# Closing the first token group of batch 0 out of SBUF, and regrouping the work around it, in a one-core FFT-mixing and MLP kernel

## The chip, the cores and the metric

The kernel runs on one core of a Trainium2 chip. The metric is the device time of one launch in microseconds; the time before is the median of five runs. A core has five engines with one instruction queue each: TensorE (PE, with its weight loads listed as PEld), VectorE (DVE), ScalarE (ACT), GpSimd (POOL) and SyncE (SP), which here only issues DMAs. POOL and ACT issue DMAs too. Every engine takes its instructions strictly in the order in which they were written; a waiting instruction holds up all that stand behind it.

## The reference, cut to what matters

```python
X = np.fft.rfft(x, axis=1)                    # x: 8 batches, 3136 tokens, 256 channels
y = np.fft.irfft(X * (filt_r + 1j * filt_i), n=3136, axis=1)   # one filter value per frequency and channel
h = y.transpose(0, 2, 1) @ U @ V              # U: 3136 x 32, V: 32 x 3136, mixes tokens
u = y + h.transpose(0, 2, 1)
out = u + np.maximum(u @ w_ch1, 0.0) @ w_ch2  # 256 -> 1024 -> 256 channels
```

Inputs and output are float32; the kernel computes in float16 with float32 accumulation.

## The kernel before, in words

The transform of length 3136 is split as 64 x 49. **Stage 1** (`st1`) is a transform of length 64 as a matmul with the constant `wf`; its result goes by DMA to a buffer `ct1` in DRAM and comes back transposed as tiles `a2` (`load_a2`). **Stage 2** is a matmul with `w2t` over the other factor. The result, in PSUM, is multiplied by the filter tiles `fb` and `fc`. **Stage 3** transforms back (`stage3`, constant `g3`), is copied to SBUF tiles `esb` (`out3`, ACT), and goes to a second DRAM buffer `ct2`, from which it returns transposed as tiles `e2` (`load_e2`, issued by SP). **Stage 4** (`stage4`) is the last transform, a matmul with `sv`. The low-rank product U V costs little here: `uh` (U transformed, made once by `u_hat`) times `esb` gives a 32 x 256 tile (`low_rank`, `low_rank_end`), which `put_h` writes into rows 64 to 95 of each `e2` tile, and V stands in the same rows of `sv`. So stage 4 gives u, transposed, in tiles `ut`.

The tokens of a batch are cut into six groups of 512 (and a remainder of 64, which two batches share). The **main loop** walks over the groups in 8 steps each. In a step `mm1` makes 128 of the 1024 hidden channels (two matmuls, one ACT activation into the ring `hring`), `stage4` prepares the next group in two of the steps, and `mm2_part` multiplies the hidden channels of the group before by `w2sb`, adds the residual (matmuls with `idn`) and stores the output. There are 52 such groups, so 416 steps.

Stages 1 to 3 of the coming batches are laid between the steps by a planner: `at(step, function)` hangs work behind a step, `early[step]` puts it ahead. `plan_mid` places stages 2 and 3 of a batch: per index k (8 of them) a load `fetch`, the matmul `two`, three DVE multiplications `mul` (into `ta` and twice into `tb`) with an addition on POOL, or, for some k, all on POOL after an ACT copy (`pooled`), then `three`. `plan_rest` places `load_e2`, `low_rank` and `put_h`; `plan_st1` places stage 1 of the batch after, in 13 units (`step1`).

Batch 0 has nothing to hide behind. Ahead of the loop its x is transformed straight into a transposed form (`turned`, `turn_a2`), with no DRAM in between; `mid_first` then runs stages 2 and 3 in 16 half units j with another form of the filter product: one multiplication per unit (L400 on DVE, or for j = 7, 9, 12, 14 an ACT copy L395 and POOL L397), and two matmuls with different constants in stage 3. After it come the loads of `e2` for the first two groups, the low-rank product, the whole of stage 1 of batch 1 (13 units, L266 with copies L271 and L273), six `keep_warm` matmuls, stage 4 of group 0 and the copies of the filters into the form that the other batches need (`make_fa`, L543 to L549).

In the listing, POOL's queue begins with U, x of batch 0 and the filters, then V, `w1sb`, x of batch 1 and `w2sb`; SP's with `wf`, `sv` and `kr`.

Of the kernel before, what the change touches and what calls it, by code (L numbers as in the profile page):

```python
# [24 lines left out]
def _consts():  # L25
# [10 lines left out]
    wf = np.zeros((128, 25, 128))  # L36
    for h in range(2):
        wf[h::2, 0:24, 64 * h:64 * h + 64] = t1[:, 24 * h:24 * h + 24]
    wf[0:64, 24, 0:64] = t1[:, 48]
# [59 lines left out]
    return (wf.reshape(128, 25 * 128).astype(f16), w2.astype(f16), g3.astype(f16),  # L99
# [4 lines left out]
def kernel(  # L104
# [13 lines left out]
    names = ("wf", "w2", "g3", "s4", "su", "tw", "kr")  # L118
    wf_d, w2_d, g3_d, s4_d, su_d, tw_d, kr_d = (
# [22 lines left out]
    def bank(tag):  # L142
        of = {"m": (0, 1), "o": (2, 3), "w": (4,), "e": (7,), "f": (0, 1, 2, 3, 4, 7), "e0": (7, 4), "f0": (0, 1), "w1": (7, 5, 6)}[tag]
        turn[tag] = turn.get(tag, -1) + 1
        return psum[:, of[turn[tag] % len(of)], :]


    NH = 17
    hring = cst.tile([128, NH, 512], F16, name="hring")
# [3 lines left out]
    wf = cst.tile([128, 25, 128], F16, name="wf")  # L153
    for c in range(4):
        i = slice(8 * c, min(8 * c + 8, 25))
        nc.sync.dma_start(wf[:, i], wf_d.rearrange("p (i m) -> p i m", m=128)[:, i])
# [3 lines left out]
    def load_x(b, c, after=None):  # L160
# [3 lines left out]
        else:  # L164

            t = sb.tile([128, 4, XW], F16, tag="x", bufs=4, name="x")
            if after is not None:
                nc.gpsimd.tensor_copy(t[0:1, 0, 0:1], after[0:1, 0:1])
# [10 lines left out]
    def load_filters(a, z):  # L179
        n = min(z, 31) - a  # L180
        for p0, src in ((0, filt_r), (64, filt_i)):
            nc.gpsimd.dma_start(
                fb[p0:p0 + 25, a:a + n, :],
                dram(src.tensor, (a + 1) * DM, [[64 * DM, 25], [DM, n], [1, DM]]))
            nc.gpsimd.dma_start(
                fb[p0 + 25:p0 + NR, a:a + n, :],
                dram(src.tensor, (63 - a) * DM, [[64 * DM, 24], [-DM, n], [1, DM]]))
        if z == NK:
            for p0, src in ((0, filt_r), (64, filt_i)):
                nc.gpsimd.dma_start(fb[p0 + 25:p0 + NR, 31, :],  # L190
                                    dram(src.tensor, 32 * DM, [[64 * DM, 24], [1, DM]]))
            nc.gpsimd.dma_start(fb[0:25, 31, :], dram(filt_r.tensor, 0, [[64 * DM, 25], [1, DM]]))
            nc.gpsimd.dma_start(fb[65:89, 31, :],
                                dram(filt_i.tensor, 64 * DM, [[64 * DM, 24], [1, DM]]))
            nc.gpsimd.dma_start(fb[64:65, 31, :],
                                dram(filt_r.tensor, 1568 * DM, [[DM, 1], [1, DM]]))

    zero = cst.tile([128, 64], F16, name="zero")
    nc.vector.memset(zero, 0.0)
    nc.vector.memset(fb[96:128], 0.0)  # L200
    nc.scalar.copy(fb[32:64].rearrange("p s (k f) -> p (s k) f", f=64),
                   free(zero, 32, 64, 0, [[0, NK * DM // 64], [1, 64]]))
    nc.vector.memset(fc[:, 24:29, :], 0.0)
    usb = hflat[0:64, 0:NR * RANK]
    nc.gpsimd.dma_start(usb, moe_U.rearrange("(q r) p -> q (r p)", q=NQ))
# [4 lines left out]

# [7 lines left out]
    nc.scalar.dma_start(g3, g3_d.rearrange("p (f m) -> p f m", f=6))  # L218

# [3 lines left out]
    w2sb = cst.tile([128, 8, DM], F16, name="w2sb")  # L223
    vnat = hflat[64:96, 4704:4704 + SEQ]
    nc.gpsimd.dma_start(vnat, moe_V)
    nc.gpsimd.dma_start(w1sb, moe_w_ch1.rearrange("(h dd) c -> dd h c", h=2))

    sv = cst.tile([96, SEQ], F16, name="sv")
    kr = cst.tile([128, 96], F16, name="kr")

    def keep_warm(n):
        z = bank("f")
        for _ in range(n):
            nc.tensor.matmul(z, wf[:, 0, :], wf[:, 0:4, :].rearrange("p i m -> p (i m)"),
                             start=True, stop=True)
# [4 lines left out]
    def u_hat():  # L240
        ud = hflat[0:64, 1568:4704].rearrange("q (p c r) -> q p c r", c=2, r=NR)
        for p, eng in ((0, nc.vector.tensor_copy), (16, nc.scalar.copy)):
            eng(ud[:, p:p + 16], bass.AP(tensor=usb.tensor, offset=usb.offset + p,
                                         ap=[list(usb.ap[0]), [1, 16], [0, 2], [RANK, NR]]))
        for p in range(0, RANK, 8):
            z = bank("f")
# [4 lines left out]
            t = [sb.tile([98, NK, 8], F32, tag=tag, bufs=3, name="ut") for tag in ("ta", "tb")]  # L251
# [8 lines left out]
    def st1(b):  # L260
        for c in range(3):
            asb = sb.tile([128, 8, DM], F16, tag="asb", bufs=3, name="asb")
            for j in range(4):
                pf = bank("w" if b > 1 else "w1")
# [5 lines left out]
                if b == 1 and j % 2:  # L270
                    nc.vector.tensor_copy(dst, pf)  # L271
                else:
                    nc.scalar.copy(dst, pf)  # L273
                if j < 3:
                    yield
            for h in range(2):
                nc.sync.dma_start(dram(ct1[b], (16 * c + h) * 64 * DM,
                                       [[DM, 64], [128 * DM, 8], [1, DM]]), asb[64 * h:64 * h + 64])
            if 1 < b < NB - 1 and c:
                load_x(b + 1, c - 1)  # L280
            yield
        pf = bank("w" if b > 1 else "w1")
        nc.tensor.matmul(pf[0:64, 0:DM], wf[0:64, 24, 0:64], xt[b, 3], start=True, stop=True)
        al = sb.tile([64, DM], F16, tag="al", bufs=2, name="al")
        nc.scalar.copy(al, pf[0:64, 0:DM])
        nc.sync.dma_start(dram(ct1[b], 48 * 64 * DM, [[DM, 64], [1, DM]]), al)
        if 1 < b < NB - 1:
# [5 lines left out]
    cm = fc.rearrange("p s d -> p (s d)")  # L293

    def turned(c):
        for g in range(0, 8 if c < 3 else 1, 4):
            for hh in range(2):
                z = bank("f")
                n, o = 512, 3136 * hh + (8 * c + g) * 128
                if c < 3:  # L300
                    for i in range(4):
                        nc.tensor.matmul(z[:, 128 * i:128 * i + 128],
                                         xt[0, c][:, (g + i) // 2, DM * (i % 2) + 128 * hh:DM * (i % 2) + 128 * hh + 128],
                                         wf[:, 8 * c + g + i, :], start=(i == 0), stop=True,
                                         skip_group_check=True)
                else:
                    n = 64
                    nc.tensor.matmul(z[:, 0:n], xt[0, 3][:, 128 * hh:128 * hh + 128],
                                     wf[0:64, 24, 0:64], start=True, stop=True)
                if hh:  # L310
# [3 lines left out]


    esb = {}
# [6 lines left out]
    def out3(b, k, half, pe):  # L323
        if half == 0:
            esb[b, k] = sb.tile([98, 4, DM], F16, tag="esb", bufs=10, name="esb")
        nc.scalar.copy(esb[b, k][:, 2 * half:2 * half + 2, :].rearrange("p s d -> p (s d)"),  # L326
                       pe[0:98])
        if half:
            nc.sync.dma_start(dram(ct2[b], 4 * k * 98 * DM, [[DM, 98], [98 * DM, 4], [1, DM]]),
                              esb[b, k])  # L330

    def stage3(pe, parts, special):

        for n, (v, m, ms) in enumerate(parts):
            kw = dict(start=(n == 0), stop=(n == len(parts) - 1))
            if special:
                nc.tensor.matmul(pe[0:98, 0:DM], g3[:, m, :], v[:, 0:DM], skip_group_check=True, **kw)
        if special:
            for n, (v, m, ms) in enumerate(parts):
                nc.tensor.matmul(pe[0:98, DM:2 * DM], g3[:, ms, :], v[:, DM:2 * DM], start=False,  # L340
                                 stop=(n == len(parts) - 1), skip_group_check=True)
        else:
            for n, (v, m, ms) in enumerate(parts):
                nc.tensor.matmul(pe[0:98], g3[:, m, :], v, start=(n == 0), stop=(n == len(parts) - 1))  # L344
# [8 lines left out]

    def mid_first():
# [3 lines left out]
        def turn_a2(k):  # L358
            z = bank("f0").bitcast(F16)
            for i in range(4):  # L360
                for hh in range(2):
                    nc.tensor.transpose(z[:, DM * i + 128 * hh:DM * i + 128 * hh + 128],
                                        free(fc, 0, 128, 3136 * hh + 4 * k + i, [[32, 128]]), idn)
# [4 lines left out]
            if k in (1, 3):  # L368
                nc.vector.tensor_copy(a2[k], z[0:98])
            else:  # L370
                nc.scalar.copy(a2[k], z[0:98])

        todo = []

        def do3(j, uv):
            pe = bank("e0")
            stage3(pe, [(uv[:, 0], 2, 4), (uv[:, 1], 3, 5)], j == 15)
            out3(0, j // 2, j % 2, pe)

        for k in range(4):  # L380
            turn_a2(k)
        for c in range(4):
            load_x(1, c)
# [384 lines left out]
```

## Time and profile before

| What | us |
|---|---|
| median of 5 runs (553.0 to 560.42) | 556.28 |
| the profiled execution's own time | 553.0 |
| its span, first to last instruction | 551.2 |
| PE busy in the span | 515.0 (93%) |
| ACT / DVE / POOL busy | 390.7 / 352.9 / 282.4 |
| first multiplication of `mid_first` (L400) | at 24.46 |
| last matmul of stage 3 of batch 0 ends | at 45.78 |
| first matmul of the main loop (L488, step 0) | at 57.29 |
| PE held for group 0 of batch 1 (stage 4, in step 46) | 122.4 to 125.96 |

All times of single instructions count from the span's start. A row of a timeline reads: start, duration, engine, line, operation, tiles, number of instructions, and in brackets the idle time before it and what ended it. "PEclk" is the share of full TensorE clock that was granted.

### The profile page before, as it was taken

To read this page: it belongs to the slowest core of one execution; us is meant where nothing else is said; L and a number is where in the kernel's file an instruction comes from. 1 tells how busy PE (TensorE), PEld (TensorE's weight loads), DVE (VectorE), ACT (ScalarE), POOL (GpSimd) and SP (SyncE) were. 2 spreads that over 40 slices of the span, in tenths; PEclk is the share of its full clock that TensorE was granted. 3 is DMA by queue.
4 is the path that set the end of the run, shared out by engine and by line. 5 is a ranking of instruction groups with operands and counts; after the bars stand their busy time and mean duration, and the time that the engine had idled before them with its cause. 6 is when DMAs were issued, how large, how long until landed. Compare 5 with 4: busy or idle time off the path is not lost.

```text
span 551.2 us, 11638 instructions
## 1 busy us (share of the span) xinstructions
PE 515.0 (93%) x4491; PEld 374.7 (68%) x4491; DVE 352.9 (64%) x409; ACT 390.7 (71%) x684; POOL 282.4 (51%) x194
## 2 busy tenths in 40 slices
PE   5976598988999999999999999999999999999996
PEld 2733366765776777777786777777776777777775
DVE  6764864864746875858746876768656887543332
ACT  8576778764777688677777678668767677766663
POOL 5787379933891185806683195807453287300000
PEclk9899999997999999999999999999999999999999
DMA  9998988886769369865878459865654554343212
GB/s 193 165 174 185 228 180 209 193 197 176 177 160 247 117 174 231 163 201 153 198 196 205 138 174 240 164 205 145 190 151 135 142 156 122 106 116 113 96 78 87
DMA packets 85432, 92.06 MB, mean 167 GB/s; under 512 B 6741, under 2 KB 69416, under 8 KB 85376
## 3 DMA queue, kind: packets, MB, share of 16 engines
q1 hardware_dynamic: 67968, 75.12, 46.2%
q0 software_dynamic: 16960, 15.91, 19.1%
q8 instruction: 35, 0.57, 0.4%
q10 hardware_dynamic: 448, 0.28, 0.3%
q14 instruction: 21, 0.17, 0.1%
HBM read 57.42 MB, written 49.77 MB: 194 GB/s over the span
## 4 chain that ended last, share of the span: by engine, by line
PE 66%; POOL 15%; DMA 7%; DVE 7%; ACT 3%; issue 2%; DVEq 0%; POOLq 0%; ACTq 0%; SPq 0%
PE psum L521 24%; PE psum L488 24%; POOL y L634 4%; PE psum L344 4%; PE psum L352 3%; PE psum L477 3%; PE psum L497 3%; PE psum L266 3%; DMA x<-in_x_dram 2%; POOL x L170 2%; POOL tb L632 2%; POOL tb L630 2%; POOL ta L628 2%; DVE ut L482 1%; DVE tb L632 1%
## 5 line engine op out<-in xcount | busy, mean ns | idle before, releaser
L492 ACT ACTIVATE hring<-psum 128x512 f16<-128x512 f32 (+1 forms) x416 | 237.7, 576 | 104.2 <-PE psum L488 103.0
L488 PE MATMUL psum<-ut,w1sb 128*128 128x512 f16 (+1 forms) x832 | 241.1, 372 | 3.5 <-ACT hring L492 1.7
L521 PE MATMUL psum<-w2sb,hring 128*128 128x256 f16 x1536 | 231.4, 274 | 0.0
L634 POOL TENSOR_TENSOR y<-ta,tb 128x1024 f16<-128x1024 f16 x56 | 120.6, 2160 | 159.2 <-DVE tb L632 115.5
L521 PEld LDWEIGHTS <-hring 128*128 128x128 f16 x1536 | 143.7, 98 | 62.6 <-issue 2.9
L482 DVE CAST ut<-psum 128x512 f16<-128x512 f32 x96 | 71.0, 740 | 106.9 <-PE psum L477 86.6
L488 PEld LDWEIGHTS <-w1sb 128*128 128x128 f16 x832 | 104.9, 145 | 26.1 <-issue 9.1
L529 DVE COPY och<-psum 128x512 f32<-128x512 f32 x96 | 66.1, 688 | 47.5 <-PE psum L497 46.9
L326 ACT CAST esb<-psum 98x512 f16<-98x512 f32 x128 | 74.7, 586 | 19.9 <-PE psum L344 14.1
L628 DVE TENSOR_TENSOR ta<-psum,fb 128x1024 f16<-128x1024 f32 x41 | 49.9, 1217 | 7.9 <-PE psum L352 6.9
L273 ACT CAST asb<-psum 128x512 f16<-128x512 f32 x78 | 45.7, 589 | 12.3 <-PE psum L266 11.2
L497 PE MATMUL psum<-idn,ut 128*128 128x128 f16 x392 | 54.0, 219 | 0.0
L477 PEld LDWEIGHTS <-e 96*128 96x128 f16 x768 | 35.6, 98 | 25.2 <-issue 9.5
L630 DVE TENSOR_TENSOR tb<-psum,fc 64x1024 f16<-64x1024 f32 x41 | 50.3, 1226 | 0.9
L632 DVE TENSOR_TENSOR tb<-psum,fc 64x1024 f16<-64x1024 f32 x41 | 49.9, 1218 | 0.8
L477 PE MATMUL psum<-sv,e 96*128 96x64 f16 x768 | 38.7, 194 | 6.3 <-DMA e<-ct 3.5
L344 PE MATMUL psum<-y,g 128*98 128x512 f16 x105 | 39.9, 380 | 2.8 <-POOL y L634 1.4
L497 PEld LDWEIGHTS <-ut 128*128 128x128 f16 x392 | 38.4, 98 | 4.9
L628 POOL TENSOR_TENSOR ta<-pc,fb 128x1024 f16<-128x1024 f16 x15 | 32.4, 2157 | 10.8 <-ACT pc L638 10.8
L352 PE MATMUL psum<-a,w2t 98*128 98x512 f16 x113 | 34.3, 379 | 3.6 <-DMA a<-ct 2.5
L266 PE MATMUL psum<-x,wf 128*128 128x256 f16 x168 | 31.3, 273 | 2.8 <-DVE asb L271 1.0
L630 POOL TENSOR_TENSOR tb<-pc,fc 64x1024 f16<-64x1024 f16 x15 | 31.8, 2122 | 1.2
(93 smaller groups left out, 368.9 us busy)
## 6 DMA issues: line engine op xcount, KB each, us to landing
out_dram<-och SPq DMA_DIRECT2D x47, 512.0 KB
ct<-esb SPq DMA_DIRECT2D x64, 196.0 KB
x<-in_x_dram POOLq DMA_DIRECT2D x48, 256.0 KB, 8.3
e<-ct SPq DMA_DIRECT2D x48, 256.0 KB
a<-ct SPq DMA_DIRECT2D x56, 196.0 KB
ct<-asb SPq DMA_DIRECT2D x42, 256.0 KB
wf<-wf SPq DMA_DIRECT2D x3, 256.0 KB
w1sb<-in_moe_w_ch_dram POOLq DMA_DIRECT2D x1, 512.0 KB, 6.0
```

The source lines that it names most:

```text
L326: nc.scalar.copy(esb[b, k][:, 2 * half:2 * half + 2, :].rearrange("p s d -> p (s d)"), pe[0:98])
L477: nc.tensor.matmul(pu[:, 64 * i:64 * i + 64], e2[b, c][:, i, 128 * dh:128 * dh + 128], sv[:, 64 * r:64 * r + 64], start=(i == 0), stop=Tru ...
L482: nc.vector.tensor_copy(o, v)
L488: nc.tensor.matmul(ph[:, 0:n], w1sb[:, dh, :, t], gr.ut[:, dh, 0:n], start=(dh == 0), stop=(dh == 1))
L492: nc.scalar.activation(h[:, 0:n], ph[:, 0:n], RELU)
L497: nc.tensor.matmul(o[:, dh * 128:dh * 128 + 128], gr.ut[:, dh, t0:t0 + n], idn, start=False, stop=(dh == 1), skip_group_check=True)
L521: nc.tensor.matmul(o, gr.h[tt][:, i * 128:(i + 1) * 128], w2sb[:, tt, :], start=(tt == 0), stop=False, skip_group_check=True)
L529: nc.vector.tensor_copy(gr.och[:, 2 * y:2 * y + 2, :].rearrange("p j d -> p (j d)"), gr.pc)
L628: eng.tensor_mul(ta, p, va)
L630: eng.tensor_mul(tb[0:64], p[64:128], vb[64:128])
L632: eng.tensor_mul(tb[64:128], p[0:64], vb[0:64])
L634: nc.gpsimd.tensor_add(ys[k], ta, tb)
```

## The change: what it does

- **Ahead of the loop.** U is read in float32 by SP rather than converted by POOL's DMA. `wf` comes in half its size and is widened by two DVE multiplications with a 0/1 column. The zero rows of `fb` are written by one DVE memset instead of one on DVE and a 7.02 us ACT copy. The transposed tiles of batch 0 get a buffer of their own (`cm`). `u_hat` is cut into parts between the `turned` calls.
- **POOL's queue.** x of batch 0 first, then filters, V, `w1sb`, the last filter rows, x(1,0) and x(1,1); the copy of V into `sv`; after `mid_first` x(1,2), `w2sb` (now with padded rows, 512 bytes each), x(1,3), and five filter copies. x(2) is read in steps 13 to 16, x(3) in steps 40 to 45.
- **mid_first.** 15 of the 16 multiplications on DVE, only j = 12 on POOL; `low_rank_part` follows each k.
- **Group 0.** Rows 0 to 47 of e2(0,0) (k = 0 to 5) are loaded from `ct2` as soon as k = 5 is stored. The other 16 rows don't go through DRAM: `pick` gathers them from `esb` with 0/1 matrices `sel` into `zp`, and one matmul per half with `s4x` adds their part of stage 4. The low-rank part is a separate matmul.
- **Stage 1 of batch 1.** Three units stand ahead of step 0, the other ten in steps 0 to 8, on two PSUM banks of their own; eight of the copies are on DVE. The last stores to `ct1` are issued by POOL.
- **Batch 1.** Its stages 2 and 3 run in steps 15 to 42 instead of 5 to 40; k = 0, 1 and 7 use the one-multiplication form of batch 0 (`two_q`, `mul_q`, `three_q`), k = 3 and 5 run on POOL. The filter copies are cut into eight parts and spread over POOL and DVE.
- Filter products run over 113 instead of 128 partitions; batch 2 has k = 1, 3, 5 on POOL instead of 2, 5.

```diff
+    usb = hflat[0:64, 0:2 * NR * RANK].bitcast(F32)
+    nc.sync.dma_start(usb, moe_U.rearrange("(q r) p -> q (r p)", q=NQ))
+    nc.sync.dma_start(wfc, wf_d)
...
+    nc.vector.memset(fb[32:64], 0.0)
...
+        def low_rank_part(k):
+            for i in range(4):
+                a = 4 * k + i
+                nc.tensor.matmul(ph[32 * i:32 * i + 32], uh[:, a, :], esb[0, k][:, i, :],
+                                 start=(k == 0), stop=(k == 7), skip_group_check=True)
+        def pick(j):
+            for i in range(2):
+                sl = 2 * (j - 12) + i
+                for g in range(4):
+                    nc.tensor.matmul(zp[32 * g:32 * g + 32], sel[:, g, 28 - 4 * sl:60 - 4 * sl],
+                                     esb[0, j // 2][:, 2 * (j % 2) + i, :], start=(sl == 0),
+                                     stop=(sl == 7), skip_group_check=True)
...
+                if k == 5:
+                    load_e2(0, 0, 48)
+                if k == 6:
+                    load_e2(0, 1, 48)
+                if k == 7:
+                    load_e2(0, 1, 64, 48)
+                    nc.sync.dma_start(sv[0:64, 512:], s4_d[:, 512:])
+                    load_e2(0, 2)
...
-            if j in (7, 9, 12, 14):
+            if j == 12:
...
+                for k in (3, 2, 5):
+                    make_fc(k, nc.gpsimd.tensor_copy)
...
+        step1(1)
+        step1(1)
+        pick(14)
+        low_rank_part(7)
+        pick(15)
...
+        for dh in range(2):
+            nc.tensor.matmul(pu[dh], zs[:, 128 * dh:128 * dh + 128], s4x, start=False, stop=False,
+                             skip_group_check=True)
+        step1(1)
...
     mid_first()
-    load_e2(0, 0)
-    load_e2(0, 1)
...
-    for n, _ in enumerate(st1(1)):
...
-    keep_warm(6)
-    stage4(groups[0], 0)
-    stage4(groups[0], 1)
...
+    load_x(1, 2)
+    nc.gpsimd.dma_start(w2sb[:, :, 0:DM], moe_w_ch2.rearrange("(cc t) e -> cc t e", t=8))
+    load_x(1, 3)
+    for k in (4, 0, 1, 6, 7):
+        make_fc(k, nc.gpsimd.tensor_copy)
...
+            for k, q in ((0, 11), (3, 11), (1, 11), (5, 11), (2, 17), (4, 20), (6, 22), (7, 25)):
+                at(q, fetch, k)
+            for k, q, d in ((3, 17, 26), (5, 21, 32), (2, 23, 34), (4, 28, 37), (6, 33, 39)):
+                at(q, two, k)
...
+            for k, qs in ((0, (15, 16)), (1, (19, 20)), (7, (38, 39))):
+                for half, q in enumerate(qs):
+                    at(q, two_q, k, half)
...
+            return 42
...
+    for n in (0, 0, 1, 1, 2, 4, 5, 6, 7, 8):
+        at(n, step1, 1)
+    at(13, lambda: load_x(2, 0, a2q[0][0:1, 0:1]))
+    for c in range(4):
+        if c:
+            at(13 + c, load_x, 2, c)
+        at((40, 42, 44, 45)[c], load_x, 3, c)
+    for n, k in ((5, 0), (5, 1), (7, 2), (8, 3), (8, 4), (9, 5), (11, 6), (11, 7)):
+        at(n, make_neg, k)
+    for n, k in ((12, 2), (12, 3), (13, 4), (13, 5), (14, 6)):
+        at(n, make_fa, k, nc.vector.tensor_copy)
+    for n, k in ((34, 0), (35, 1), (41, 7)):
+        at(n, make_fa, k, nc.gpsimd.tensor_copy)
```

## The prediction

> **What bounds the kernel now.** I read the page's row of slices first, then the busy time by stretches cut where the stages change, then the chain of waits in the two stretches where PE is not full.
>
> ```profile
> PE   5976598988999999999999999999999999999996
> PEclk9899999997999999999999999999999999999999
> DMA  9998988886769369865878459865654554343212
> ```
>
> PE is full from about slice 10 on: nothing gains there that doesn't take work off PE. It is not full in the first five slices (0 to 69 us) and in slice 9 (124 to 138 us), where the clock drops too. The stretches (length, then busy us of PE, PEld, DVE, ACT, POOL, granted clock, DMA share, GB/s):
>
> ```profile
> 0.00:24.46 24.46, 17.16 (x135) 11.40 (x136) 16.79 (x25) 16.83 (x12) 15.98 (x31) 0.86 1.05 186
> 24.46:45.78 21.32, 17.21 (x98) 9.35 (x98) 14.29 (x13) 15.52 (x23) 17.96 (x20) 1.00 1.03 174
> 45.78:57.29 11.51, 7.17 (x82) 4.45 (x81) 5.68 (x8) 7.96 (x13) 5.92 (x1) 1.00 0.73 188
> 57.29:68.20 10.91, 6.08 (x42) 3.25 (x39) 9.88 (x18) 8.11 (x11) 4.96 (x8) 0.93 0.88 219
> 68.20:121.83 53.63, 50.99 (x431) 36.41 (x430) 35.27 (x38) 41.61 (x76) 42.33 (x25) 0.98 0.87 203
> 121.83:131.90 10.07, 6.12 (x42) 3.78 (x39) 6.18 (x8) 2.28 (x5) 0.00 (x0) 0.66 0.42 101
> 131.90:500.00 368.10, 363.37 (x3245) 269.25 (x3244) 248.31 (x279) 271.07 (x499) 195.21 (x111) 1.00 0.64 171
> ```
>
> They are: the start, bound by DMA (share 1.05); `mid_first`; the handover to the loop; group 0 (DVE 9.88 of 10.91); steps 8 to 46, near PE's limit; the stall for batch 1; the steady part. The chain shows the two handovers:
>
> ```profile
> 46.02 1.08 PE psum L416 x32
> ...
> 54.35 1.46 PE psum L234 x6
> ...
> 55.83 0.42 PE psum L477 x8
> ...
> 57.49 0.73 DVE ut L482
> ...
> 115.83 6.37 DMA ct<-esb
> ...
> 122.34 3.48 DMA e<-ct
> ...
> 125.96 0.60 PE psum L477 x8
> ```
>
> After the low-rank matmuls (46.02) ten microseconds pass with stage 1 of batch 1 before stage 4 of group 0. The second handover is a store (6.37) and a load (3.48) on which PE waits. Who sets the first one if stage 1 leaves it, SP's rows tell:
>
> ```profile
> 30.00 16.79 SPq L329 DMA_DIRECT2D ct<-esb  x8
> 52.13 1.10 SPq L438 DMA_DIRECT2D e<-ct  x2
> ```
>
> The last store is out at 46.8 and the load leaves at 52.13: 5.3 us.
>
> **The parts.** All sums are made against the profiled execution: 553.0, span 551.2.
>
> *Start, to the first multiplication: -2.3 us.* Until the last x tile (which POOL saw at 18.36) the queues moved about 200 GB/s. `wf` loses 0.41 MB and `sv`'s 0.40 MB wait, against 0.2 MB more for U and 0.18 MB for `sel` and `s4x`: 0.43 MB less, 2.1 us; x leaves POOL 0.7 us earlier; filter pieces that slip in earlier take some back. I take the last x at 17.0. Behind it the two extra `turn_a2` go (-1.2 us), but a part of `u_hat` stands on DVE there (1.08 + 0.42): first multiplication at 22.2. Bounds 0 and -4.
>
> *mid_first: -0.4.* 15 DVE multiplications at 1.22 plus one 0.69 copy are 19.0; with gaps of 0.68 as at the POOL units of before, and stage 3 of the last unit, 20.9 instead of 21.32. Losing three POOL units at 2.12 thus gains little: DVE takes their place. Its end: 43.1.
>
> *First handover: 11.51 becomes 6.9, -4.6.* The load of 48 rows hangs on j = 11, whose `esb` is stored at about 40.6. The store takes between 2.2 (the small store `al` of before, out at 60.36, its reader off at 62.6) and 5.3; I take 3.0, because the 5.3 ran through a backlog (the queues fell idle only at 51), while here some 7.3 MB, at 200 GB/s, are through by 39. Load 3.5 (row of 122.34): 47.1. Then 16 small matmuls 0.45, `s4x` 0.86, a unit of stage 1 0.22, the low-rank matmuls 0.43, the copy 0.73, and 0.2 of issue: step 0 at 50.0, not 57.29. The path beside it (`pick`, `low_rank_part`, two copies of 0.37, `kr`) ends at 45.6 and is hidden; the three stage 1 units need x(1,0) by 43, which those 7.3 MB include. Bounds: 48.5 and 52.3.
>
> *Group 0: 10.91 becomes 9.5, -1.4.* DVE gets seven stage 1 copies (0.69), two `ut` copies (0.73), two `put_h` (0.69) and three `make_neg` (half of L544's 0.69): 8.7 us. ACT loses its filter copies (1.89 each) and PE's ten units (2.2 us) fit beside. Three arrivals stand close: the second group's e2(0,1), whose last 16 rows pass a store, a load, a store and a load on SP in a row (about 53.7, needed in step 4 at 54); x(1,2), behind one multiplication and three copies on POOL; and w2sb behind it. A POOL copy of 49 x 1024 has no row; L634 with two inputs takes 2.12 and is the upper bound, DVE's 0.35 the lower; I take 1.6, nearest to L634. Then x(1,2) leaves at about 46 and w2sb at 48, needed in step 8 at 59.5. Before, w2sb took 14.7 from issue to landing behind seven x transfers (1.6 MB, some 8 us); here one tile stands ahead: about 9. Five more copies (8 us) stand ahead of batch 1's last stores on POOL; their chain (3 us out, 3.9 back) ends at 65, step 15 comes at 66.9. At 2.12 a copy it costs 2.1 us.
>
> A row bears on POOL and DVE working side by side: while POOL's 6.94 us copy (L562, to 51.71) ran, DVE's `put_h` took 0.89 instead of 0.68. The Trainium skill (SBUF — State Buffer, "SBUF: two separate sides") calls the port pair of the two an exclusive lock: the later one waits for the whole instruction. By that rule some five DVE copies of group 0 would each wait up to one POOL copy, about half on average, and the time would be some 4 us higher. I keep the row, 0.2 us each.
>
> *Steps 8 to 46: 53.63 becomes 53.2.* The one-multiplication form of k = 0, 1, 7 costs PE four more 0.215 matmuls per k: +2.6. Against it: the 2.64 us in which PE was not busy, mostly waiting for ACT and for POOL's additions; one pooled k less (8.5 us of POOL) and 5 us less of ACT copies should give back 2.0; and the clock of 0.67 in 65 to 70 us, worth 1.0 after 68.2. Bounds -2 and +3.
>
> *Second handover: +2.2.* Stage 3 of batch 1 now ends in step 42, not 40, while stage 4 stays in step 46; two steps at 1.1. The way itself (115.02 to 125.96, 10.9 us) I leave: x(3,0) and three `fetch` are issued right ahead of that store and load the queues as x(3) did before. Bounds: -2 (the store at 2.2) and +4.
>
> The Trainium skill (DMA: Bandwidth & Descriptors, "Anatomy of one DMA") gives a DMA as 2.0 us plus bytes over 436 GB/s, an estimate of 2.5 us for this 196 KB store. The rows say 5.3 and 6.37, under load. By the page the second handover would be 3.9 us shorter and the first 1.5, and the time about 544.
>
> *Steady part: 0.* The work is the same; 113 partitions don't change an instruction's length that a row would show, and batch 2's third pooled k finds POOL at 195 of 368 us.
>
> Sum: -2.3 - 0.4 - 4.6 - 1.4 - 0.4 + 2.2 = -6.9. The profiled execution would take 546.1. The median lies 3.3 above the profiled run, so I set the median at **549.3**, rounded to 549.
>
> **Rivals.**
> - *Clean handovers (0.24).* Both stores land in 2 to 3 us. For: DMA share 0.64 later, and 0.05 at 51 to 52 us. Against: 1.04 at 112 to 120. Gain 6.9 + 1.5 + 3.9: 544 (541 to 545.5).
> - *The gain is given back (0.18).* Store at 5.3 (+2.3), POOL copies at 2.12 (+2.1): 554 (552.5 to 557). That includes that the first group isn't closed early at all, because x(1,0) is late and the stage 1 units ahead of `pick` hold PE.
> - *w2sb comes last (0.11), slower than before.* Its read goes behind x(1,2) and POOL's copies and is cut into 1024 rows of 512 bytes instead of 128. If it takes twice the 14.7, it lands at 77 and holds step 8 for 18 us: 567. It costs from 59.5 on, eats the gain at 66, and is over 1% slower from 72. Against: the x tiles, in rows of 1 KB, come at 1.3 us for 256 KB, so small rows need not double it.
>
> **How the numbers follow.** The forecast has 0.47 (545.5 to 552.5). One percent, 5.6 us, is about what a measurement can tell: faster is below 550.7. Faster: 0.24 and four fifths of the forecast, 0.62. Within 1%: the rest of it and the second rival, 0.27. Slower: 0.11. The range 541 to 557 leaves out the last rival and little else.
>
> **What would show it.** Step 0 (the first `mm1` matmul) near 50; the first multiplication near 22; a gap of PE ahead of stage 4 in step 46 of 5 to 6 us with a clock below 0.7 behind it; no gap at step 8 or 15. I am wrong if step 0 comes after 53, or if PE stands at step 4, 8 or 15 for more than 3 us, or if the steps of batch 1 wait for POOL's `y`.

## The result, and the profile after

The changed kernel takes **560.33 us** (median of 43 runs, 556.69 to 565.9) against 556.55 for the kernel before on the same chips (80 runs): ratio 1.0063, 95% interval 1.0049 to 1.0076. It is slower by 0.6%, within the one per cent that the prediction called no change; 549 was forecast and 557 was the end of the range.

The profiled execution after took 562.41 us, span 560.6. It lies 2.1 us above its median, while the one before lay 3.55 below its own. The two profiles are therefore 9.4 us apart where the medians are 3.8 apart; the stages below are read from the profiles, the worth of each edit from the ratios.

Rows of slices of the page of after:

```profile
PE   5869979966999999999999999999999999999996
PEclk9995989987999999999999999999999999999999
DMA  9997688595689556785779468775753544243212
```

The thin place of PE has stayed in slices 8 and 9 (112 to 140 us), and behind it nothing is new. Busy time by stretches, cut at the first multiplication, the last matmuls of `mid_first`, step 0, step 8 and stage 4 of batch 1 (length, then busy us of PE, PEld, DVE, ACT, POOL, granted clock, DMA share, GB/s):

```profile
0.00:20.69 20.69, 12.73 (x119) 8.06 (x119) 16.03 (x25) 10.49 (x14) 14.57 (x27) 1.00 1.02 187
20.69:46.67 25.98, 21.72 (x149) 11.10 (x147) 18.02 (x16) 14.12 (x21) 21.35 (x22) 0.90 0.83 158
46.67:53.81 7.14, 6.64 (x57) 2.91 (x56) 2.29 (x5) 2.48 (x5) 5.88 (x7) 0.50 1.12 175
53.81:63.61 9.80, 8.73 (x52) 5.11 (x51) 6.75 (x12) 6.01 (x11) 0.00 (x0) 0.76 0.90 211
63.61:134.44 70.83, 56.98 (x442) 38.65 (x442) 42.31 (x52) 40.84 (x74) 41.01 (x36) 0.95 0.76 178
134.44:145.00 10.56, 10.56 (x76) 7.11 (x77) 5.46 (x8) 5.56 (x9) 6.88 (x4) 0.72 0.49 138
```

Step 0 comes at 53.81 (before 57.29) and step 8 at 63.6 (before 68.2): the start did gain, 3.5 to 4.6 us. Then 70.83 us pass until stage 4 of batch 1, where before 57.76 did (68.20 to 125.96). From there to the end it is 426.2 us after and 425.2 before. **The whole loss lies between step 8 and step 46.** Four times PE stood for over 2 us behind the first multiplication; PE's timeline, with the idle time and what ended it in brackets:

```profile
41.92 1.01 PE L381 MATMUL psum<-uv,g 113*98 113x512 f16 x2 [3.68 <-POOL uv L482]
...
74.26 0.59 PE L389 MATMUL psum<-a,w2t 98*128 98x512 f16 x2 [2.44 <-DMA a<-ct]
...
122.41 0.59 PE L389 MATMUL psum<-a,w2t 98*128 98x512 f16 x2 [4.21 <-DMA a<-ct]
...
134.44 0.59 PE L588 MATMUL psum<-sv,e 96*128 96x64 f16 x8 [5.16 <-DMA e<-ct]
```

The rows are the end of `mid_first`, step 15 (first stage 2 of batch 1), step 42 (first stage 2 of batch 2) and step 46 (stage 4 of batch 1). Two of them had a counterpart before: step 46 one of 3.53 us, and the first stage 2 of batch 1 one of 2.55 us, then in group 0. PE's timeline of before:

```profile
65.70 0.59 PE L352 MATMUL psum<-a,w2t 98*128 98x512 f16 x2 [2.55 <-DMA a<-ct]
```

What stands behind them is in the chain of work that ended last, of after:

```profile
31.43 1.22 POOL x L187 x2
...
32.70 6.98 POOL sv L468
...
39.75 2.12 POOL uv L482
...
47.56 7.64 DMA ct<-esb
...
55.62 4.01 DMA sv<-s
...
67.11 0.70 POOL ct L303
67.81 3.57 DMA ct<-al
71.40 2.82 DMA a<-ct
...
118.85 11.78 DMA ct<-esb
130.68 3.62 DMA e<-ct
```

In order: the copy of V into `sv` holds POOL for 6.98 us, and the one multiplication left to POOL (j = 12) comes behind it; the store of k = 7 takes 7.64, and `sv`'s rest, which SP reads only after it, feeds step 4; step 15 hangs on the store of `al` and a load; and the last store of batch 1 takes **11.78 us**, where the same store took 6.37 before. What SP and POOL issue around it, in SP's and POOL's timelines of after:

```profile
115.11 2.94 SPq L352 DMA_DIRECT2D a<-ct  x3
118.10 1.16 SPq L366 DMA_DIRECT2D ct<-esb  x2
```

```profile
112.64 1.30 POOL L187 DMA_DIRECT2D x<-in_x_dram  x2
...
117.99 2.45 POOL L187 DMA_DIRECT2D x<-in_x_dram  x4
```

Batch 2's `a2` loads leave at 115.1, right ahead of the store, and two tiles of x(3) (x4 is two halves of each) leave on POOL within the same two microseconds as the store. Before, these two tiles had left ten microseconds ahead of it (115.83), as POOL's timeline of before shows:

```profile
105.28 2.54 POOL L170 DMA_DIRECT2D x<-in_x_dram  x4
```

The late loads and the tiles gave the theory: the loads of `a2` come too late for step 42 because they leave only three steps ahead, and x(3) beside the last store doubles it for step 46. The rival was that the store is slow for other reasons (the loads of `a2` ahead of it), or that the waits only mirror the late start.

### The profile page after: what moved, and what is told of

Same layout as the page of the kernel before. It is cut to its first block, busy times and chain, and to the rows that moved or that the text cites. A ratio compares the mean times of both kernels' runs of the same rounds, so it can differ in the third digit from the quotient of the medians.

```text
span 560.6 us, 11718 instructions
## 1 busy us (share of the span) xinstructions
PE 524.4 (94%) x4531; PEld 375.9 (67%) x4531; DVE 353.9 (63%) x415; ACT 375.7 (67%) x678; POOL 284.6 (51%) x204
## 4 chain that ended last, share of the span: by engine, by line
PE 76%; DMA 7%; POOL 5%; DVE 4%; ACT 3%; issue 2%; SPq 0%; ACTq 0%; DVEq 0%; POOLq 0%
PE psum L632 27%; PE psum L599 26%; PE psum L389 5%; PE psum L381 5%; PE psum L588 4%; DMA ct<-esb 3%; PE psum L608 3%; PE psum L295 3%; POOL sv L468 1%; POOL y L731 1%; DMA a<-ct 1%; PE psum L526 1%; ACT esb L359 1%; DVE uv L754 1%; DVE tb L729 1%
## 5 line engine op out<-in xcount | busy, mean ns | idle before, releaser
L731 POOL TENSOR_TENSOR y<-ta,tb 113x1024 f16<-113x1024 f16 x53 | 114.2, 2160 | 148.8 <-DVE tb L729 116.7
L593 DVE CAST ut<-psum 128x512 f16<-128x512 f32 x94 | 69.6, 740 | 102.6 <-PE psum L588 90.8
L725 DVE TENSOR_TENSOR ta<-psum,fb 113x1024 f16<-113x1024 f32 x38 | 46.3, 1217 | 15.7 <-PE psum L389 14.2
L727 DVE TENSOR_TENSOR tb<-psum,fc 49x1024 f16<-49x1024 f32 x38 | 46.6, 1226 | 0.9
L729 DVE TENSOR_TENSOR tb<-psum,fc 49x1024 f16<-49x1024 f32 x38 | 46.3, 1218 | 1.0
L389 PE MATMUL psum<-a,w2t 98*128 98x512 f16 x118 | 36.5, 387 | 9.3 <-DMA a<-ct 6.6
L725 POOL TENSOR_TENSOR ta<-pc,fb 113x1024 f16<-113x1024 f16 x15 | 32.3, 2154 | 19.2 <-ACT pc L735 19.1
L381 PE MATMUL psum<-y,g 113*98 113x512 f16 x100 | 38.2, 382 | 2.0 <-ACT esb L359 1.0
L295 PE MATMUL psum<-x,wf 128*128 128x256 f16 x168 | 33.6, 287 | 0.3
L187 POOL DMA_DIRECT2D x<-in_x_dram x48 | 30.5, 648 | 5.3 <-PE psum L381 4.1
```

Of the source, the lines that this page charges most:

```text
L381: nc.tensor.matmul(pe[0:98], g3[0:NZ, m, :], v, start=(n == 0), stop=(n == len(parts) - 1))
L389: nc.tensor.matmul(pz, w, a, start=True, stop=True)
L593: (nc.scalar.copy if gr is groups[0] and dh else nc.vector.tensor_copy)(o, v)
L725: eng.tensor_mul(ta, p[0:NZ], va)
L731: nc.gpsimd.tensor_add(ys[k], ta, tb)
```

## The experiments

Ratios are to the kernel before; after itself is 1.0063. One hundredth is 5.6 us.

**The copy of V ahead of the second x tile.** POOL's issue of x(1,1) waits, and V's copy stands behind it; here the copy goes first.

```diff
         load_x(1, 0)
-        load_x(1, 1)
         nc.gpsimd.tensor_copy(sv[64:96, :]...)
+        load_x(1, 1)
```

> One edit to the changed kernel: POOL's copy of V into sv stands ahead of the issue of x(1,1) instead of behind it. Theory A (POOL's queue in mid_first): the copy starts at about 28 instead of 32.7, ends at 35, the one POOL multiplication (j = 12) starts at 36 instead of 39.75, PE's idle 3.7 us ahead of stage 3 of j = 12 goes, the clock does not drop to half behind it, step 0 comes at about 48 instead of 53.8, and the time falls by 4 to 7 us to 553 to 556. Rival B (a later wait takes it over): step 0 comes earlier as under A, but the waits for a2 and e2 of batch 1 grow by what the front gained, and the time stays within 2 us of 560. Rival C (the added matmuls on PE are the cause): no wait matters, time within 1 us of 560.

Measured: 558.25, ratio 1.0033 (1.0004 to 1.0061), 1.7 us less than after by the ratios, where the first theory had 4 to 7. The copy ran at 28.0 instead of 32.7 and j = 12 at 36.4; the gap of 3.68 us is gone. PE's timeline has another in its place, for the 48 rows of e2(0,0):

```profile
47.33 1.03 PE L506 MATMUL psum<-sv,e 48*128 48x64 f16 x16 [3.54 <-DMA e<-ct]
```

Step 8, counted here and below by its first matmul with `w2sb`, came at 61.1, against 63.8 after; the waits in steps 15, 42 and 46 stayed (2.47, 4.13, 3.86). The order on POOL is a cause, and a small one; the pair of versions under "Combinations" shows it again.

**Batch 2's steps later.** The low-rank and stage 2 steps of batch 2 stand six steps later in the plan, with their loads. This kernel leaves something out: `put_h` for batch 2 then comes after the first half of its group 0, which uses batch 1's low-rank rows.

```diff
-        m = later(start[b - 1], (16, -6, -12)[min(b, 3) - 1])
+        m = later(start[b - 1], (16, 0, -12)[min(b, 3) - 1])
```

> One edit: stages 2 and 3 of batch 2 start in step 48 instead of 42, so that its first loads of a2 leave in step 45 instead of 39. Theory A (the transfers of batch 2 collide with the handover to batch 1): the wait of 4.2 us at step 42 goes (stage 1 of batch 2 ends in step 37 and its loads have three steps), the three loads no longer stand ahead of the last store of batch 1, and the time falls by 3 to 6 us. Rival B: the wait for e2 in step 46 grows by what the wait in step 42 gave back, because that store lands no earlier: within 1.5 us of the changed kernel. Rival C (PE work): within 1 us.

Measured: 565.43, ratio 1.018 (1.0124 to 1.0237). The wait in step 42 is gone, the one in step 46 has grown, and batch 2 now ends too late for its own stage 4. PE's timeline:

```profile
129.91 0.58 PE L588 MATMUL psum<-sv,e 96*128 96x64 f16 x8 [9.16 <-DMA e<-ct]
...
197.11 0.61 PE L588 MATMUL psum<-sv,e 96*128 96x64 f16 x8 [4.52 <-DMA e<-ct]
```

The store ahead of step 46 still kept its reader for 10.4 us, with no `a2` load ahead of it. So the loads of `a2` are not what makes it slow; that rival fell.

**x(3) later.** The last three tiles of x(3) leave in steps 47, 53 and 54.

```diff
-        at((40, 42, 44, 45)[c], load_x, 3, c)
+        at((40, 47, 53, 54)[c], load_x, 3, c)
```

> One edit: x of batch 3, parts 1 to 3, is read in steps 47, 53 and 54 instead of 42, 44 and 45. Theory A: the last store of batch 1, which took 11.8 us from issue to its reader, lands in 5 to 7 us since 1 MB less lies in the queues beside it; the 5.2 us wait in step 46 shrinks to below 1 us and the half clock behind it goes; the time falls by 5 to 8 us. Rival B: the store is held by the a2 loads and the output store on its own queue, not by x; the wait stays over 4 us and the time within 1.5 us.

Measured: 565.53, ratio 1.0184 (1.0099 to 1.027): the time missed, the mechanism held. SP waited 5.7 us for the last store, and the wait in step 46 is gone. But x now stands on POOL behind four operations of a pooled k (130.0 to 139.4), and PE waits for it:

```profile
147.20 0.59 PE L295 MATMUL psum<-x,wf 128*128 128x256 f16 x2 [7.21 <-DMA x<-in_x_dram]
```

**x(3) held just until the load has landed.** All three tiles are written at step 45, ahead of the pooled k, and a one-element copy from e2(1,0) makes POOL wait for it.

```diff
-        at((40, 42, 44, 45)[c], load_x, 3, c)
+        if c:
+            at(45, lambda c=c: load_x(3, c, e2[1, 0][0:1, 0, 0:1] if c == 1 else None))
+        else:
+            at(40, load_x, 3, c)
```

> One edit: parts 1 to 3 of x of batch 3 are issued by POOL only once e2(1,0), the tile that PE waits for in step 46, has landed (a one-element copy from that tile holds the queue), ahead of the pooled product of batch 2. The same cause as in the kernel that read them in steps 47 to 54, without the late x that cost that kernel its gain. Theory A (x of batch 3 holds the store): the store takes 5 to 6 us instead of 11.8, the wait in step 46 falls from 5.2 to below 1.5 us, x(3,1) is there before step 52, and the time falls by 4 to 7 us to 553 to 556. Rival B (what is taken away here comes back at the next stage of batch 2): within 1.5 us of the changed kernel.

Measured: 555.77, ratio 0.9996 (0.9959 to 1.0032): about 3.7 us below after, level with the kernel before. SP's waits for the last store (us in total, times, longest), of after and of this kernel:

```profile
SPq L548 <- DMA ct<-esb: 11.4, 1, 11.4
```

```profile
SPq L548 <- DMA ct<-esb: 5.5, 1, 5.5
```

The stage 4 of batch 1 began at 127.25 without a wait for its data. Over all thirteen profiles of this study the row reads 10.4 to 11.8 in the five where x(3) leaves beside the store, 5.5 to 6.2 in the seven where it is held or later, and 6.1 before. **x(3) beside the store is shown as the cause of its doubling.** The wait in step 42, 4.71 us here, is another matter.

**Matmuls to keep the clock.** After the 3.68 us gap TensorE runs at 0.50 until step 0 and at 0.76 in group 0. Eighteen extra matmuls ahead of stage 3 of j = 12 fill the gap.

```diff
+            if j == 15:
+                for _ in range(18):
+                    nc.tensor.matmul(psum[:, 4, :], cm[:, 6784:6912], cm[:, 6272:6784], start=True, stop=True)
             while len(todo) > (3 if 11 < j < 15 else 2) or todo and j == 15:
```

> One edit: 18 matmuls of 512 columns on zeros stand in PE's queue ahead of stage 3 of j = 12, where PE idles 3.7 us; they change no result. It parts the wait from the half clock behind it (0.50 in 47 to 54 us, 0.76 in 54 to 64). If the half clock costs, step 0 comes 2 to 3 us earlier (51 to 52) and the time falls by 2 to 4 us; if the stretch is bound by copies, loads and stores, step 0 moves by less than 1 us and the time by less than 1 us.

Measured: 561.12, ratio 1.0101 (1.0041 to 1.0161). The clock was 1.00 from 41 to 55 us and step 0 came at 50.80, three microseconds earlier; step 8 came at 66.09, two *later*. The interval doesn't part this time from that of after. PE's timeline says where it went:

```profile
60.19 0.58 PE L591 MATMUL psum<-sv,e 96*128 96x64 f16 x8 [4.52 <-DMA sv<-s]
```

Step 4 needs the rest of `sv`, and that hangs on SP's row of store (46.87 to 55.19), two loads and `sv` itself. Behind that wait the clock fell to 0.50 again (62 to 65 us), so this run doesn't price the half clock by itself. What it shows is that an earlier step 0 meets SP's row next. Four other profiles agree (batch 2 later above, and the last three versions below): step 0 came at 47.2 to 48.1, PE then waited 2.0 to 3.8 us for `sv`, and step 8 came at 60.2 to 61.6. In none of the twelve profiles of the changed kernel and its versions did it come earlier.

**No selection matmuls.** `pick`, `zs` and the early loads of 48 rows go; group 0 waits for the whole of e2(0,0), as before the change, with all else left as it is.

```diff
-                if k == 5:
-                    load_e2(0, 0, 48)
-                if k == 6:
-                    load_e2(0, 1, 48)
...
-                    load_e2(0, 1, 64, 48)
+                    load_e2(0, 0)
+                    load_e2(0, 1)
...
-        pick(14)
-        pick(15)
```

> The first group closed the old way in the changed kernel: no selection matmuls, e2(0,0) and e2(0,1) loaded whole after the store of k = 7, the low-rank rows written by put_h, stage 4 as in all other groups. It tells what the selection matmuls alone are worth. By the changed kernel's rows (store out at 47.6, its reader off at 55.3, load 3.6, stage 4 and copies 1.5) step 0 comes at 60 to 61 instead of 53.8; since stage 4 of group 1 waits for the same store anyhow (59.7), 2 to 4 us of the 6 come back in group 0, and the time rises by 2 to 5 us. If it rises by less than 1 us, the title's part of the change is worth nothing as things stand.

Measured, with two runs: 568.12, ratio 1.0203 (1.0122 to 1.0285), 7.8 us above after. Stage 4 of group 0 waited for the load, and step 0 came at 56.50:

```profile
54.63 0.58 PE L565 MATMUL psum<-sv,e 96*128 96x64 f16 x8 [8.12 <-DMA e<-ct]
```

The idea at the core of the change has a worth that is clear of noise: even the near ends of the two intervals lie 2.6 us apart. That it is worth more than the 2 to 5 us forecast is not shown: the interval is wide, and the two profiles are 4.1 us apart (566.52 and 562.41), not 7.8. The loss must then lie in what was moved along with it.

**Combinations.** First, the edits for V and x(3) with batch 2's steps three later and their loads six steps ahead, one pooled k moved with them (called the three edits); then the same without the edit for V.

```diff
-        m = later(start[b - 1], (16, -6, -12)[min(b, 3) - 1])
-        z = plan_mid(b, m, (2, 5) if b > 2 else (1, 3, 5))
+        m = later(start[b - 1], (16, -3, -12)[min(b, 3) - 1])
+        z = plan_mid(b, m, (2, 5) if b > 2 else (1, 3, 6 if b == 2 else 5))
...
-            at(later(s, -3 if b == 2 else -9), fetch, k)
+            at(later(s, -6 if b == 2 else -9), fetch, k)
```

> Three edits to the changed kernel: the copy of V ahead of x(1,1); x(3,1) to x(3,3) held until e2(1,0) has landed; and stages 2 and 3 of batch 2 start in step 45 with loads still in step 39, with k = 1, 3, 6 on POOL so that they end early enough. Theory A (three waits made the change slower, and its front gain is real): no wait of 4 us in step 42, at most 3 us in step 46, step 0 near 51; the time is 549 to 553, below the kernel before (556.4). Rival C (the extra matmuls of the one-multiplication form and the packed steps 15 to 42 ate the gain): the time stays above 555.

> The same without the move of the copy of V: only x of batch 3 held and batch 2 three steps later. Theory A: 551 to 555, that is 1 to 3 us above the kernel with all three, which is what the wait in mid_first and its half clock are worth once nothing behind takes it over. If the move of the copy of V is worth nothing there (rival B), the two agree within 1 us.

Measured: 554.16, ratio 0.9962 (0.9932 to 0.9993), and 556.37, ratio 0.9991 (0.9964 to 1.0018). The expected 549 to 553, with at most 3 us of waiting in step 46, was missed. V's copy is worth 2.2 us between the two medians, 1.6 by the ratios. In both, the wait in step 42 is gone and step 46 waits 5.3 and 5.1 us, though SP waited only 6 us for the last store. So the wait in step 46 had come back without x(3) beside the store. And the second version is no faster than the one with x(3) held alone, measured beside it (556.37 and 555.77): moving batch 2's steps gained nothing that these runs resolve. To settle which of the two waits it is that costs, the same with batch 2's steps where the change put them:

> V copy ahead of x(1,1) and x(3,1..3) held until e2(1,0) has landed, but batch 2's low-rank and stage 2 steps where the change put them. Theory (the wait of 4 to 5 us for a2 of batch 2 in step 42 and the 5 us wait for e2(1,0) in step 46 are paid from the same transfers, so that removing one while the other stays gains what the larger of the two costs and no more): the wait in step 42 stays at 4 to 5 us, none over 1.5 us in step 46, and the time is that of the version with all three edits, 554.2, within 1. Rival (each wait has a price of its own, so that moving batch 2's steps was worth its 4 us by itself and the 5.3 us wait there came from elsewhere): 557 to 558.

Measured: 553.10, ratio 0.9953 (0.9933 to 0.9973): level with the three edits (0.5 us below by the ratios), as the first theory had it. PE's timeline has the one wait of this version, in step 42, and of the version with batch 2 later and SP's stores (below), in step 46:

```profile
121.97 0.91 PE L389 MATMUL psum<-a,w2t 98*128 98x512 f16 x2 [4.41 <-DMA a<-ct]
```

```profile
124.22 0.59 PE L588 MATMUL psum<-sv,e 96*128 96x64 f16 x8 [5.35 <-DMA e<-ct]
```

Stage 4 of batch 1 needs a store and a load behind stage 3's end, about 10 us in all. In these versions PE waits for a part of that time either in step 42 or in step 46, and the lead of batch 2's loads chooses where. An earlier end of batch 1's stage 3 would give both more room; that wasn't tried.

Last, the stores that step 15 waits for go to SP, without and with batch 2's steps later:

```diff
-                (nc.gpsimd if (b, c) == (1, 2) else nc.sync).dma_start(dram(ct1[b], ...
+                (nc.gpsimd if (b, c, h) == (1, 2, 0) else nc.sync).dma_start(dram(ct1[b], ...
...
-        (nc.gpsimd if b == 1 else nc.sync).dma_start(dram(ct1[b], 48 * 64 * DM, ...
+        nc.sync.dma_start(dram(ct1[b], 48 * 64 * DM, ...
```

> As c4_sv_x3, and the last half of the third store of batch 1's stage 1 and the store of its remainder al go out on SP instead of POOL. Theory (step 15 waits for a2(1,0) because al is issued on POOL at 67.8 behind the two big stores, lands at 71.4 and the load takes 2.8): the wait of 2.4 us in step 15 is under 0.5 us, and the time is 1.5 to 2.5 us below c4_sv_x3. Rival (the load of a2(1,0) hangs on ACT's al copy and on the queues' load, not on POOL's issues): step 15 still waits 2 us or more, the time within 0.7 of c4_sv_x3.

> The three edits together (V copy ahead of x(1,1), x(3,1..3) held until e2(1,0) has landed, batch 2's steps three later with loads six steps ahead) and the two stores of batch 1's stage 1 on SP. Theory: 1.5 to 2.5 us below the version with three edits (554.2), 552 to 553, no wait in step 15, the 5 us wait in step 46 unchanged. Rival (what step 15 gains is lost in step 46, where the handover ends by its own chain of store and load): within 0.7 of 554.2, with the wait in step 46 about 2 us longer.

Measured: 552.76, ratio 0.9931 (0.9904 to 0.9958), and 552.68, ratio 0.9944 (0.9925 to 0.9964). Both theories missed half: the wait in step 15 fell to 1.4 and 1.5 us (from 1.7 and 2.4 in the versions that they start from), not below 0.5, and the gain over the versions with the stores on POOL is 1.2 and 1.0 us by the ratios (0.3 between the medians of the first pair, which ran side by side), less than the intervals resolve. What the wait in step 15 costs stays open. In the first, the chain now runs through the half store left on POOL (61.91, its reader off at 66.69 instead of 67.77). These two are the fastest here: 0.6 to 0.7% below the kernel before, 1.2 to 1.3% below after.

That is still 3.4 us above the 549.3 forecast. Where the rest of the start's gain went, the busy time between step 8 and stage 4 of batch 1 tells, of before and of the last version (columns as above):

```profile
68.61:125.96 57.35, 51.19 (x432) 36.46 (x431) 35.91 (x39) 42.12 (x76) 42.33 (x25) 0.98 0.84 196
```

```profile
60.45:124.22 63.77, 54.02 (x443) 37.60 (x442) 36.77 (x49) 40.85 (x75) 34.61 (x28) 1.00 0.73 182
```

Step 8 comes 8.2 us earlier and stage 4 of batch 1 only 1.7. Of the 6.4 us between, 2.8 are PE's busy time (54.02 against 51.19; the forecast had 2.6 for the one-multiplication form) and 3.3 are waits (1.48 in step 15 and 5.35 in step 46, against 3.53).

## Why the prediction was wrong

By its own steps, against the profiled execution (546.1 forecast, 562.4 measured; of these 16.3 us, 11.0 remain between the medians):

| Step | forecast | measured | difference |
|---|---|---|---|
| first multiplication at | 22.2 | 20.69 | -1.5 |
| `mid_first` | 20.9 | 26.2 (to 46.9) | +5.3 |
| first handover | 6.9 | 6.9 (to 53.81) | 0 |
| group 0 | 9.5 | 9.8 | +0.3 |
| step 8 to stage 4 of batch 1 | 59.6 (57.76 - 0.4 + 2.2) | 70.83 | +11.3 |
| the rest | 425.2 | 426.2 | +1.0 |

- **The start** was right in sign and better than forecast.
- **mid_first** failed. The step counted POOL's losses of work as gains and placed its one multiplication as at the POOL units of before. It left out POOL's queue ahead of j = 12: the issue of x(1,1) waits, then V's copy runs 7 us. POOL's timeline of the version with x(3) held names what it waits for (in after the issue stands at 31.43 behind 4.11 us of idle time, and the profile names a matmul, L381, instead):

```profile
29.96 1.22 POOL L187 DMA_DIRECT2D x<-in_x_dram  x2 [3.25 <-DMA w1sb<-in_moe_w_ch_dram]
31.23 6.96 POOL L468 COPY sv<-hring 32x3136 f16<-32x3136 f16 x1
38.27 2.12 POOL L482 TENSOR_TENSOR uv<-pc,fb 113x1024 f16<-113x1024 f16 x1
```

  `w1sb` had been issued on the same queue, eight DMAs earlier. In all seven profiles with this order the issue begins 0.53 us after `w1sb` has landed, in after's too (30.90 and 31.43). In the trace POOL's DMAs raise eight semaphores in turn, and the issue of x(1,1) waits for the one that `w1sb` raises: the wait is written in the program. The prediction priced w2sb's way on this queue and not this one. A part of the 5.3 us is the clock: from 41.92 to 46.91 PE was busy throughout at 0.50, an estimate of 2.5 us lost. The gap varies between executions: PE's wait was 3.68 us in after's, 1.50 in that one, and 0.82 in the version with batch 2 later, whose start is the same code; there the clock stayed at 1.00 and step 0 came at 48.11, which is part of why after's profile overstates the loss.
- **First handover**: the length was right by accident. The early load was forecast to land at 47.1, and where PE waited for it (V's copy first) it let PE go at 47.33; the half clock stretched the small matmuls behind it, which the forecast had at full clock, and `mid_first` ended late enough to hide the load. The point "wrong if step 0 comes after 53" came true (53.81).
- **Group 0** was right in length, 9.5 and 9.8, with no wait over 0.2 us for `sv` in step 4, but by luck: step 0 came late and at a clock of 0.76. Where step 0 came at 47.2 to 48.1, the group took 12.4 to 13.5 us, with PE waiting for `sv` in step 4. The sum had the arrival of `sv`'s rest nowhere, and the store of k = 7 ahead of it on SP took 7 to 8 us. A POOL copy of 49 x 1024 took 1.0 us, not 1.6. w2sb came 9.9 us after its issue, forecast 9, and nobody waited for it: the rival of the slower side fell with its price.
- **Steps 8 to 46 at -0.4** is the step that failed most. Its sum had no wait at all in it. Steps 15 and 42 waited 2.44 and 4.21 (6.7 us together); the first is the wait for the first `a2` of batch 1, which before stood in group 0 (2.55 us). The credits of 2.0 for fewer short waits and 1.0 for the clock mostly didn't come: short waits add up to 2.0 us where before they were 2.6, and the clock behind the two new gaps fell to 0.82 (74 to 84 us) and 0.75 (122 to 129), 1.8 and 1.7 us, worth 3.5 instead of the 0.9 that the same stretch lost before. The 2.6 us more of matmuls did come. Of the 11.3 us, 6.7 are thus the two waits, 3.8 are PE's busy time beyond the forecast (56.98 against 51.59 + 2.6 - 1.0), 1.4 are short waits, and 0.6 came back because step 46 waited less than forecast. For step 15 the estimate had the chain ready at 65 with step 15 at 66.9; it was ready at 74.2 with step 15 at 71.8. The chain's start was the error: it put the stores on POOL where its copies end, while they wait for stage 1 itself (`al` was copied at 64.7), and only then come two issues of 1.1 us each, 3.57 out and 2.82 back. Batch 2's loads, three steps ahead where the later batches have nine, had no term at all. The runs show that wait and where it can be moved to; no price of its own was measured.
- **The rivals.** Clean handovers fell with both stores (7.64 and 11.78, not 2 to 3). The gain was given back, as the second rival has it, but neither by the store at 5.3 nor by POOL's copies, and further than to its 554.
- **Second handover, +2.2.** The size of the wait was near (5.16, forecast 5.7, with the clock at 0.72 behind it as foretold), by the wrong path. The prediction left the way itself at 10.9 us because x(3) was to load the queues "as x(3) did before". But it counted only x(3,0), and the tiles of steps 42 and 44 leave beside the store, where before they left ten microseconds ahead. The store alone grew by 5.4 us, and PE met it twice: 4.21 us of waiting in step 42 lie under the same store. The bound of +4 for this term was too small for the two together.

A rule was weighed twice in the prediction. The Trainium skill (DMA: Bandwidth & Descriptors, "Anatomy of one DMA") fits a DMA that POOL issues as 2.0 us plus bytes over 436 GB/s; carried over to this 196 KB store on SP's queue, as the prediction did, that is an estimate of 2.5 us. Measured were 5.5 to 6.2 us of waiting with x held and up to 11.8 with it beside. The rows decided rightly against the rule, but even the row of before did not hold once the neighbours changed.

The rule on the shared port (SBUF — State Buffer, "SBUF: two separate sides": the engine that starts first has the port pair for its whole instruction, and the other waits) had no price in group 0 of after's profile, where POOL's eight copies ended at 52.6, before DVE's `ut` and `put_h` copies began at 53.0. Where they met there, it shows, as in DVE's and POOL's timelines of the version with batch 2 later:

```profile
48.09 1.54 DVE L555 COPY e<-h 32x2048 f16<-32x2048 f16 x1
```

```profile
46.07 5.44 POOL L395 COPY fc<-fb 49x1024 f16<-49x1024 f16 x5
```

The same `put_h` takes 0.69 alone (at 53.79 in after), and the five copies 4.96. Of the five, one ended at 49.07; `put_h`, begun at 48.09, ended 0.55 later, and the copy behind it took 1.51 us instead of 1.03. Later it shows in after itself:

```profile
128.21 2.37 DVE L555 COPY e<-h 32x2048 f16<-32x2048 f16 x1 [0.48 <-ACT h L536]
```

```profile
127.91 2.11 POOL L731 TENSOR_TENSOR y<-ta,tb 113x1024 f16<-113x1024 f16 x1 [7.47 <-PE psum L295]
```

Here `put_h` ends 0.56 after POOL's addition does, as if it had begun only then; the wait for the load covered it. The row of before, from which the prediction took its 0.2 us, was misread: that `put_h` (51.36, 0.89 us) began only 0.35 us before POOL's copy ended at 51.71, and ended 0.54 after it. The rule agrees with all three rows, and the 0.2 us that the prediction kept does not. What it costs the whole kernel, no run here shows.

## What to carry to other kernels

A store and load on which the next stage waits should have no bulk transfer beside it: the same store took half the time when prefetches of another batch were held for ten microseconds, and holding them is a one-element copy; but they must be written ahead of long work on their queue, or they come late themselves. When a change shifts one pipeline, lay the whole queue of each engine in order (with the DMA issues that wait) and check the lead of every neighbouring pipeline's loads: here two prefetched tiles beside a store (3.7 us) and one copy behind a waiting issue (about 2 us) cost more between them than the start had gained. And look for the wait behind the one that an edit takes away: batch 2's loads, three steps ahead, made a wait of 4 us that was plain to see, and taking it away gained nothing measurable, because the next wait took its place.

## What was not expected of the hardware

- A DMA issue on POOL waited 3.25 and 4.11 us in two profiles, until `w1sb`, eight issues earlier on that queue, had landed (7.3 and 8.2 us after its own issue). All that stood behind on POOL waited with it. The trace has the wait on a semaphore that the two DMAs share; that the chip itself limits the DMAs in flight is not shown.
- A store issued behind a backlog came through about when the queues ran empty, not earlier. Before, the DMA share in steps of 2 us fell from 0.92 to 0.23 at 120, and the store's reader was off at 122.2; after, it fell from 1.12 to 0.46 at 128 (reader off at 130.7); with x(3) held, from 0.54 to 0.01 at 122 (122.8). So what counted in these three is all that was issued until then, also what was issued beside the store on another queue. What sets the order inside stays open.
- After a gap of 3.68 us of PE the granted clock stayed at 0.50 through 46.67 to 53.81, while PE was 93% busy with small work. With eighteen matmuls in the gap it was 1.00 to 55 us. Over the twelve profiles of the changed kernel and its versions, the clock ahead of step 0 fell to 0.50 in all seven in which PE, from 38 us on, had stood for 1.46 to 3.68 us in one piece, and in one of the five in which no gap there reached 0.9 us; why in that one stays open. The same start code gave both: the version with V and x(3) edited had no such gap and step 0 at 48.06, the one with V alone waited 3.54 us (the row of 47.33) and had it at 51.11. Step 8 came at 60.8 and 61.1 in the two all the same.
